# Second head mixing in seven chunks of 64 keys instead of eight of 56 and 64 columns

## The chip, the cores and the metric

The kernel runs on one core of a Trainium2 chip. The metric is the device time of one execution in microseconds. Three executions of the kernel before took 852.56, 857.35 and 858.68 us; the median is 857.35 us. The profiled execution, from which all rows below come, took 857.05 us.

## The reference

Talking-heads attention, then an MLP with SiLU, in float32. B = 4 batches, 12 heads, 448 positions, head size 64; the MLP has 1792 rows, 768 inputs and 2048 hidden units (its weights come as float64).

```python
scores = scale * np.matmul(q, k.transpose(0, 1, 3, 2))
scores = np.einsum('bhij,hg->bgij', scores, w_pre)        # first mixing of the heads
attn = np.exp(scores - np.max(scores, axis=-1, keepdims=True))
attn = attn / (np.sum(attn, axis=-1, keepdims=True) + 1e-09)
attn = np.einsum('bhij,hg->bgij', attn, w_post)           # second mixing of the heads
attn = np.matmul(attn, v)
...
h = x @ w_in                                              # x: attn, heads side by side
return (h * (1.0 / (1.0 + np.exp(-h)))) @ w_out
```

The order in which the 448 keys are held is free, as long as the scores and the values have them in the same order: the maximum, the sum and the product with `v` all run over the keys.

## The kernel before

**Stages.** The attention comes first, up to about 436 us. In its course the MLP's float64 weights are turned into float32 by a generator (`convert`, lines 38 to 100), whose loads and stores (`cw`, `cg`) share the DMA queue of SP with the attention's. Then comes the MLP (lines 629 and 645 on PE), which the change doesn't touch.

**Groups and pairs.** The queries of a batch are cut into tiles of 120 or 100 rows. Within one, a group is 2 x 5 query rows: a half of its 128 partitions holds (row, head) pairs of five rows, 60 of 64 partitions used. There are 184 groups, worked through in 92 pairs. The main loop (from line 695) goes over the groups, in a written order for each step:

- `scores` (line 339) makes scores of two heads; ACT and DVE copy them out of PSUM (`st`), and SP's DMA rearranges them into `g` (line 351), where a partition is a (row, head).
- `mix_pair` (line 399) is the first mixing, in four quarters of the PE array, 64 rows by 64 columns each: rows r of the array belong to one half of the partitions, columns c to one half of the output. DVE takes the negative maximum (line 405), ACT the exponential with its sum (line 409), into `e`, 128 x 448.
- `bound_sums`, `norm_pair` (lines 418 to 425) make 1/sum on DVE and, on POOL, `wr`: the weights of the second mixing over the sum.
- `mix_pair_again` (line 437) is the second mixing: the stationary operand is a piece of `e` (64 rows by 64 or 56 keys), the moving one is `wr` (64 x 60). A matmul of float32 is recorded as two instructions. For each of the two groups of a pair and each of `NJ` = 4 blocks of 112 keys there are four matmuls, one in each quarter: rows `s`, columns `c`. Column half `c` = 0 takes 64 keys, of which the last 8 are not its own, half 1 takes the next 56. The output `pa` has two banks of PSUM, one for each `s`.
- `put_pair` (line 446) copies `pa` out on ACT into `at`: 120 partitions hold 56 keys, 8 rows of a gap and 56 keys.
- `values` (line 368) multiplies `at` by `v`, 120 rows for each of four blocks; the gap rows of `v` are zeroed.

**Keys and values in SBUF.** Keys come by `load_k_pair` (line 249), 112 partitions of four keys each, are transposed on PE by `prep_k` (line 269) against the identity and split into two parts, `kh` on ACT and `kl` on DVE. Partition p holds keys 4p to 4p + 3, so column j * 112 + p of the transposed keys is key 4p + j. Values come by `load_v_quad` (lines 251 to 261), four heads at once, in two transfers of 56 partitions. The same four tiles `v4` also serve as the landing place of keys, so the gap rows, partitions 56 to 63 (zeroed as 32 to 63), are zeroed on POOL again when keys have been there since (line 256).

**Order.** All loads of the attention are issued by SP, in order of the program; `put` (line 469) fixes the step at which each is issued, some steps ahead of its use. On PE, POOL, DVE and ACT the order is the program's too.

Of the kernel before, what the change touches and what calls it, by code (L numbers as in the profile page):

```python
# [8 lines left out]
F32 = mybir.dt.float32  # L9
# [13 lines left out]
def raw(ap):  # L23

    return ap.bitcast(F32)
# [78 lines left out]
def talking_heads_then_silu_mlp(  # L104
# [11 lines left out]
    nc = tc.nc  # L116
    ctx.enter_context(tc.manual_schedule())
    B, H, S, D = q.shape
# [3 lines left out]
    RH = R // 2  # L122
    GP = 128
    HP = GP // 2
    GH = RH * H
    G0 = HP - GH
    JT = 112
    NJ = S // JT
    JH = JT // 2
    KV = 64 + JH  # L130
    HH = H // 2
    TQ = 12 * R
    LEAD = 4
# [15 lines left out]
    ident = const.tile([128, 128], F32, name="ident")  # L149
# [18 lines left out]
    def pool(name, bufs, stack=ctx, **kw):  # L168
        return stack.enter_context(tc.tile_pool(name=name, bufs=bufs, **kw))
# [5 lines left out]
    v2_p = pool("v2", 4, late, side="right")  # L175
    a_p = pool("a", 2, late, side="right")
# [16 lines left out]
    pa = ps_a.tile([128, 2, 512], F32, name="pa", tag="pa")  # L193
    turns = []

    def bank(p, name):
        if p is ps_a:
            turns.append(name)
            return pa[:, len(turns) % 2]
        return p.tile([128, 512], F32, name=name, tag="bank")  # L200

    v_tiles = [v2_p.tile([KV, 4, NJ, D], F32, name="v4", tag="v4") for _ in range(4)]
    zeroed = []
    g_tiles = [p.tile([GP, 12, S], F32, name="g", tag="g") for p in g_ps]

    def load_weights():
# [31 lines left out]
    def load_k_pair(b, h, queues=(nc.sync, nc.sync)):  # L238
        if h >= 4 if b == 0 else h // 4 != 1:
            x = (b * H + 8) // 4 % 4 if b else h // 4 - 1  # L240
            if x in zeroed:
                zeroed.remove(x)
            t = v_tiles[x][:JT, h % 4:h % 4 + 2].rearrange("p i j d -> p (i j d)")
            t = t.rearrange("p (j i d) -> p j i d", i=2, j=NJ)
        else:
            t = nat.tile([JT, NJ, 2, D], F32, name="kn", tag="kn")
        kns[b, h] = t
        for i in range(2):
            queues[i].dma_start(out=t[:, :, i, :], in_=k[b, h + i].rearrange("(p j) d -> p j d", p=JT))

    def load_v_quad(b, h):
        x = (b * H + h + 8) // 4 % 4
        t = v_tiles[x]
        if x not in zeroed:
            zeroed.append(x)
            nc.gpsimd.memset(t[32:64], 0.0)
        src = v[b, h:h + 4].rearrange("i (c p j) d -> c p i j d", c=2, p=JH)
        for c in (1, 0):
            nc.sync.dma_start(out=t[64 * c:64 * c + JH], in_=src[c])
        for i in range(0, 4, 2):  # L260
            vs[b, h + i] = t[:, i:i + 2]


    def prep_k(b, h):

        pt = bank(banks[0], "pt")
        kn = kns.pop((b, h))
        for j in range(NJ):
            nc.tensor.transpose(pt[:, j * JT:(j + 1) * JT], kn[:, j].rearrange("p h d -> p (h d)"), ident[:JT, :JT])

        kh, kl = ks[b, h] = [k2_p.tile([128, S], F32R, name=x, tag=x) for x in ("kh", "kl")]

        def take_high():
            nc.scalar.copy(out=kh, in_=pt[:, :S])

        def take_low():
            nc.vector.tensor_sub(out=kl, in0=pt[:, :S], in1=raw(kh))
        return [(take_high, take_low)]
# [101 lines left out]
    class Group:  # L380
# [47 lines left out]

        def mix_pair_again(self, other):

            for x, g in enumerate((self, other)):
                half = pa[:, :, x * 256:x * 256 + NJ * GH]
                for j in range(NJ):
                    for s, c in ((0, 0), (1, 1), (0, 1), (1, 0)):
                        rows = slice(HP * s, HP * (s + 1))
                        m = JH if c else 64
                        nc.tensor.matmul(  # L437
                            half[64 * c:64 * c + m, s, j * GH:(j + 1) * GH],
                            lhsT=g.e[rows, j * JT + c * JH:j * JT + c * JH + m], rhs=g.wr[rows], start=True, stop=True)

        def put_pair(self):
            if self.slot == 0:
                ats[self.n] = a_p.tile([KV, NJ, H, TQ], F32, name="at", tag="at")
            o, np, p = self.place()
            o += 2 * p * R
            nc.scalar.copy(  # L446
                out=ats[self.n].rearrange("p j g t -> p (j g) t")[:, :, o:o + 2 * R].rearrange("p x (c i) -> p x c i", i=RH),
                in_=pa[:KV].rearrange("p s (g w) -> p (s g) w", g=2)[:, :, :NJ * GH].rearrange("p c (x i) -> p x c i", i=RH))

    seq = [(b, ti) for b in range(B) for ti in range(len(tiles))]  # L450
    kns, qns, ks, vs, qs, gs, ats = {}, {}, {}, {}, {}, {}, {}
# [9 lines left out]
    at = lambda i: groups[i] if 0 <= i < len(groups) else None  # L461
# [13 lines left out]
    for n in range(1, len(seq)):  # L475
        p0, p1 = first[n - 1], first[n]
        spread = (0, 0, 0, 0, 2, 2) if n == 1 else (-6, -5, -4, -2, -1, 0) if p1 - p0 == 12 else (-6, -5, -4, -3, -2, -1)
        for h in range(0 if n > 1 else 2 * NE, H, 2):
            i = p0 + spread[h // 2]
# [7 lines left out]
    for n, (b, ti) in enumerate(seq):  # L487
        if n:
            p0 = first[n - 1]
            if n > 2:  # L490
                put(first[n - 2], lambda n=n: load_q(n)[0](), lead=7, w=2.1)
            for hg, i in ((0, p0 - 9), (1, p0 - 8)):
                if n > 1:
                    put(i, prep_q, n, hg)
            if ti == 0:
                c0 = first[n - 2]
                for h, i, lead in zip(range(0, H, 2), (0, 1, 3, 5, 7, 9), (10, 10, 11, 12, 5, 6)):
                    put(c0 + i, load_k_pair, b, h, lead=lead, w=1.2)
                    put(c0 + i, prep_k, b, h)
        if ti == 0:  # L500
            for h in range(0, H, 4):
                put(first[n] + ((5, 6, 8) if n else (15, 16, 18))[h // 4], load_v_quad, b, h, lead=2, w=1.8)
# [10 lines left out]
    def keep_busy(n):  # L513
        p = bank(ps_a, "busy")
        for _ in range(n):
            nc.tensor.matmul(p[:, :128], lhsT=ident, rhs=ident, start=True, stop=True)
# [9 lines left out]
    for h in range(0, 6, 2):  # L526
        load_k_pair(0, h, (nc.sync, nc.scalar))
    loads[1]()
    for h in range(6, H, 2):
        load_k_pair(0, h)  # L530
    steps = [(prep_q, 0, 0), (prep_k, 0, 0), (prep_k, 0, 2)]
    for h in range(0, H, 2):
        if h + 4 < H:
            steps.append((prep_k, 0, h + 4))
        steps += [(scores, 0, h)]
        if h == 0:
            steps.append((prep_q, 0, 1))
# [3 lines left out]
    for j, (what, *args) in enumerate(steps):  # L541
# [12 lines left out]
        if (what, *args) == (scores, 0, H - 2):  # L554
            for put_scores in second:
                put_scores()
    banks[:] = [ps_m]
    keep_busy(2)
    for i in range(0, LEAD, 2):
        at(i).mix_pair(at(i + 1), (ps_p, ps_m)[i // 2])  # L560
# [29 lines left out]
    def used(j):  # L590

        if j < 7 * NP:
            m, p = divmod(j, NP)
            return step_of["i", m, 0, 0], step_of["i", m, NU - 1, (4 * p + 3) // HC]
        m, f = divmod(j - 7 * NP, HF)
        return step_of["o", m, f // 2, 0], step_of["o", m, f // 2, NT2 - 1]

    for j in range(WB, len(parts)):
        s = max(used(j - WB)[1] + 1, used(j)[0] - 10)
# [80 lines left out]
    for f in range(HF):  # L680
        for m in range(7):
            if m:
                s = step_of["o", m - 1, f // 2, 0] + NT2 + 3 * (f % 2)
            else:
                s = o0 - 7 + 3 * f if f < 2 else o0 + NT2 * (f // 2 - 1) + 3 * (f % 2)
# [9 lines left out]
    for i in range(len(groups) + 1):  # L695
        g, new, old = at(i), at(i + LEAD), at(i - 1)
# [189 lines left out]
    for s, (kind, m, u, a) in enumerate(steps):  # L886
# [15 lines left out]
        p = None  # L902
        if kind == "o":
            if u == 0:
                accs[a] = bank(ps_h, "ph") if a < 4 else ps_t.tile([128, 512], F32, name="pt", tag="pt")
            p = accs[a]
            product(s, p)
        elif s >= len(phs):
            p = bank(ps_h, "ph")
# [18 lines left out]
        if kind == "i":  # L928
            n = u * HF + a
# [29 lines left out]
```

## Time and profile before

| | |
|---|---|
| median of 3 executions | 857.35 us |
| profiled execution | 857.05 us, span 855.3 us |
| PE busy | 811.6 us (95%) |
| PE weight loads | 661.6 us (77%) |
| DVE busy | 625.6 us (73%) |
| ACT busy | 511.0 us (60%) |
| POOL busy | 428.5 us (50%) |
| DMA | 132.90 MB, mean 155 GB/s |
| granted clock, mean | 0.986 |

An engine's busy time is the time in which at least one of its instructions ran; instructions that run side by side in quarters of the PE array count once. Weight loads (PEld) overlap matmuls. "Idle before" is the idle time of the engine ahead of an instruction, with what ended it. The chain of waits goes back from the last instruction to what released it, step by step; a work's share of it is the time that the end hung on that work. SPq is the queue on which SP issues transfers.

### The profile page before, as it was taken

What the parts mean: (1) busy time and instruction counts of PE and PEld (TensorE: products, weight loads), DVE (VectorE), ACT (ScalarE), POOL (GpSimd) and SP (SyncE); (2) the same over time, 40 slices, a digit from 0 to 9 for tenths busy, and PEclk for the clock granted to TensorE, in tenths of its full rate; (3) what the DMA queues carried; (4) which work ended last, traced back from release to release, by engine and by line L of the source; (5) the groups of instructions that cost most, each with busy time, mean ns of one, the idle gap of its engine ahead of it and who ended that gap; (6) DMA issues with size and microseconds to landing.
All of it is one profiled execution on the core that took longest, in us unless ns stands there. A gap on an engine that the chain in (4) does not pass through costs nothing.

```text
span 855.3 us, 27555 instructions
## 1 busy us (share of the span) xinstructions
PE 811.6 (95%) x11148; PEld 661.6 (77%) x11148; DVE 625.6 (73%) x1137; ACT 511.0 (60%) x1114; POOL 428.5 (50%) x693
## 2 busy tenths in 40 slices
PE   7898999799998999999899999999999999999997
PEld 5455666467665666666599999998989999999996
DVE  5553867467775777675778798999998888787343
ACT  4675878578886888787756554224676533433330
POOL 6131536355553554563877588457644435433440
PEclk9899999899999999999999999999999999999999
DMA  8668678887788786875535346335522122111133
GB/s 172 185 181 190 189 207 232 211 207 208 209 238 225 217 216 203 239 232 160 182 117 177 124 148 200 109 105 154 154 71 66 56 73 90 52 55 56 56 121 130
DMA packets 156839, 132.90 MB, mean 155 GB/s; under 512 B 52164, under 2 KB 150448, under 8 KB 156712
## 3 DMA queue, kind: packets, MB, share of 16 engines
q1 hardware_dynamic: 154339, 129.29, 53.3%
q8 instruction: 88, 1.44, 0.7%
q10 hardware_dynamic: 1956, 1.19, 0.6%
q0 software_dynamic: 416, 0.66, 0.3%
q14 instruction: 40, 0.32, 0.1%
HBM read 64.01 MB, written 27.53 MB: 107 GB/s over the span
## 4 chain that ended last, share of the span: by engine, by line
PE 71%; DVE 12%; DMA 6%; ACT 4%; issue 3%; POOL 2%; SPq 1%; ACTq 1%; DVEq 0%; POOLq 0%
PE ph L645 17%; PE ph L629 12%; PE pt L629 9%; PE pa L437 9%; PE po L368 7%; PE pp L399 7%; PE pqk L339 7%; DMA g<-st 3%; DVE op L652 2%; ACT e L409 1%; DVE nm L405 1%; DVE g L836 1%; DVE cg L92 1%; ACT at L446 1%; DVE g L838 1%
## 5 line engine op out<-in xcount | busy, mean ns | idle before, releaser
L616 POOL TENSOR_TENSOR wl<-wl,wh 128x384 fp32r<-128x384 f32 (+1 forms) x98 | 144.1, 1487 | 124.7 <-ACT wh L615 119.7
L425 POOL TENSOR_SCALAR wr<-wpost,r 128x60 f32<-128x60 f32 x184 | 72.7, 409 | 179.2 <-DVE r L422 131.6
L405 DVE TENSOR_REDUCE nm<-pp 128x1 f32<-128x448 f32 x184 | 106.1, 619 | 75.1 <-PE pp L399 74.6
L645 PE MATMUL ph<-op,wh 128*128 128x448 f32 x672 | 155.6, 367 | 2.7 <-DVE g L846 1.8
L409 ACT ACTIVATE e<-pp,nm 128x448 f32<-128x448 f32 x184 | 115.6, 633 | 46.6 <-DVE nm L405 44.0
L645 PEld LDWEIGHTS ph<-op,wh 128*128 128x128 f32 x672 | 125.3, 188 | 15.6 <-DVE g L846 2.1
L437 PEld LDWEIGHTS pa<-wr,e 64*64 64x64 f32 (+1 forms) x5888 | 96.4, 131 | 47.4 <-issue 29.2
L437 PE MATMUL pa<-wr,e 64*64 64x60 f32 (+1 forms) x5888 | 108.5, 218 | 16.7 <-ACT at L446 7.4
L66 POOL TENSOR_TENSOR cg<-cw,cg 128x256 f32<-128x256 f32 x96 | 75.7, 788 | 73.8 <-DVE cw L63 70.6
L399 PE MATMUL pp<-g,wpre 64*64 64x448 f32 x736 | 102.4, 573 | 8.3 <-ACT e L409 5.6
L446 ACT COPY at<-pa 120x960 f32<-120x960 f32 x92 | 90.0, 978 | 3.5 <-PE pa L437 3.5
L368 PE MATMUL po<-at,v 120*64 120x120 f32 (+1 forms) x1536 | 89.0, 271 | 2.1 <-DMA v<-in_v 1.2
L368 PEld LDWEIGHTS po<-at,v 120*64 120x64 f32 x1536 | 78.5, 141 | 15.4 <-issue 6.6
L645 PE MATMUL ph<-op,wl 128*128 128x448 f32 x336 | 86.6, 366 | 0.0
L344 DVE COPY st<-pqk 120x448 f32<-120x448 f32 (+1 forms) x89 | 54.8, 617 | 34.3 <-PE pqk L339 19.2
L90 ACT ACTIVATE cg<-cg,ebias 128x256 int32<-128x256 int32 x96 | 49.6, 517 | 39.8 <-DVE cg L86 38.6
L615 ACT CAST wh<-wl 128x384 fp32r<-128x384 f32 (+1 forms) x98 | 52.1, 556 | 33.1 <-DMA wl<-wi_dram 26.1
L92 DVE SCALAR_TENSOR_TENSOR cg<-cw,cg 128x256 int32<-128x256 int32 x96 | 55.4, 577 | 18.0 <-ACT cg L90 17.7
L645 PEld LDWEIGHTS ph<-op,wl 128*128 128x128 f32 x336 | 63.0, 188 | 5.5 <-POOL wl L616 0.5
L339 PEld LDWEIGHTS pqk<-kh,qh 64*120 64x120 f32 (+1 forms) x186 | 18.8, 174 | 43.2 <-issue 15.9
L346 ACT COPY st<-pqk 120x448 f32<-120x448 f32 (+1 forms) x89 | 48.1, 540 | 6.5 <-DMA g<-st 4.9
L399 PEld LDWEIGHTS pp<-g,wpre 64*64 64x64 f32 x736 | 23.2, 133 | 33.2 <-ACT e L409 14.5
(141 smaller groups left out, 1621.9 us busy)
## 6 DMA issues: line engine op xcount, KB each, us to landing
g<-st SPq DMA_DIRECT2D x132, 210.0 KB
cw<-in_moe_w_in SPq DMA_DIRECT2D x48, 256.0 KB
cw<-in_moe_w_out SPq DMA_DIRECT2D x48, 256.0 KB
wi_dram<-cg SPq DMA_DIRECT2D x24, 448.0 KB
wo_dram<-cg SPq DMA_DIRECT2D x24, 448.0 KB
wl<-wi_dram SPq DMA_DIRECT2D x42, 256.0 KB
wl<-wo_dram SPq DMA_DIRECT2D x56, 192.0 KB
g<-st SPq DMA_DIRECT2D x48, 175.0 KB
```

Source lines behind the costliest of these rows:

```text
L66: nc.gpsimd.tensor_mul(out=e, in0=m, in1=e)
L339: nc.tensor.matmul(ps[i][:m, :S], lhsT=q_[rows, hh, :m], rhs=k_[rows], start=(step == 0), stop=(step == 2))
L368: nc.tensor.matmul(po[i * D:(i + 1) * D, c * m:(c + 1) * m], lhsT=vs[b, h][:, i, j, :], rhs=ats[n][:, j, h + i, :m], start=(j == 0), stop= ...
L399: nc.tensor.matmul((self, other)[r].p[HP * c:HP * (c + 1), :S], lhsT=wpre[rows], rhs=gs[self.n][rows, o // R + c * np + p, :], start=True, ...
L405: nc.vector.tensor_reduce(out=self.nm, in_=self.p[:GP, :S], axis=AX.X, op=ALU.max, negate=True)
L409: nc.scalar.activation(out=self.e, in_=self.p[:GP, :S], func=AF.Exp, bias=self.nm, scale=1.0, accum_out=sums)
L425: nc.gpsimd.tensor_scalar(out=g.wr, in0=wpost.rearrange("p g i -> p (g i)"), scalar1=r[:, i:i + 1], scalar2=1.0, op0=ALU.mult, op1=ALU.mult)
L437: nc.tensor.matmul(half[64 * c:64 * c + m, s, j * GH:(j + 1) * GH], lhsT=g.e[rows, j * JT + c * JH:j * JT + c * JH + m], rhs=g.wr[rows], s ...
L446: nc.scalar.copy(out=ats[self.n].rearrange("p j g t -> p (j g) t")[:, :, o:o + 2 * R].rearrange("p x (c i) -> p x c i", i=RH), in_=pa[:KV] ...
L616: nc.gpsimd.tensor_sub(out=wl, in0=raw(wl), in1=raw(wh))
L629: nc.tensor.matmul(p[:, :W2], lhsT=x, rhs=w, start=(g == 0 and n == 0), stop=(g == FG - 1 and n == len(todo) - 1))
L645: nc.tensor.matmul(p[:, :T], lhsT=w, rhs=x, start=(n == 0), stop=(n == len(todo) - 1))
```

## The change

The keys are cut into seven chunks of 64. Chunks 0 to 2 lie on column half 0, chunks 4 to 6 on half 1, and chunk 3 on half 0 for the first group of a pair and on half 1 for the second. So the last four matmuls of a pair, one in each quarter, do chunk 3 of both groups, and a pair has 28 matmuls, not 32. The places of `pa` that belong to chunk 3 and are not written (half 1 of the first group, half 0 of the second) are zeroed once at the start, by two memsets on DVE; the copy takes them along, so `at` has zeros there. `at` and the tiles of values have 128 partitions. Chunk 3 of the values is in both halves of a tile, so a quad comes in three transfers, and no rows have to be zeroed.

The order of the keys changes with it: value partition p of a half holds keys 7p + n, chunk n. Keys are now loaded with 112 consecutive keys for each j, partition p holding key 112j + p; the transposes write their columns with a stride, so that key 7p + n stands at column 64n + p.

```diff
-    JH = JT // 2
-    KV = 64 + JH
+    KC = S // 64
...
-    v_tiles = [v2_p.tile([KV, 4, NJ, D], F32, name="v4", tag="v4") for _ in range(4)]
-    zeroed = []
+    v_tiles = [v2_p.tile([128, 4, NJ, D], F32, name="v4", tag="v4") for _ in range(4)]
...
     def load_k_pair(b, h, queues=(nc.sync, nc.sync)):
...
-            queues[i].dma_start(out=t[:, :, i, :], in_=k[b, h + i].rearrange("(p j) d -> p j d", p=JT))
+            queues[i].dma_start(out=t[:, :, i, :], in_=k[b, h + i].rearrange("(j p) d -> p j d", p=JT))
 
     def load_v_quad(b, h):
         x = (b * H + h + 8) // 4 % 4
         t = v_tiles[x]
-        if x not in zeroed:
-            zeroed.append(x)
-            nc.gpsimd.memset(t[32:64], 0.0)
-        src = v[b, h:h + 4].rearrange("i (c p j) d -> c p i j d", c=2, p=JH)
-        for c in (1, 0):
-            nc.sync.dma_start(out=t[64 * c:64 * c + JH], in_=src[c])
+        src = v[b, h:h + 4].rearrange("i (p n) d -> p i n d", n=KC)
+        nc.sync.dma_start(out=t[64:, :, :NJ - 1], in_=src[:, :, NJ:])
+        nc.sync.dma_start(out=t[64:, :, NJ - 1], in_=src[:, :, NJ - 1])
+        nc.sync.dma_start(out=t[:64], in_=src[:, :, :NJ])
...
     def prep_k(b, h):
...
+        cols = pt[:, :S].rearrange("p (n j a) -> p j a n", n=KC, j=NJ)
         for j in range(NJ):
-            nc.tensor.transpose(pt[:, j * JT:(j + 1) * JT], kn[:, j].rearrange("p h d -> p (h d)"), ident[:JT, :JT])
+            nc.tensor.transpose(cols[:, j], kn[:, j].rearrange("p h d -> p (h d)"), ident[:JT, :JT])
...
         def mix_pair_again(self, other):
 
-            for x, g in enumerate((self, other)):
-                half = pa[:, :, x * 256:x * 256 + NJ * GH]
-                for j in range(NJ):
-                    for s, c in ((0, 0), (1, 1), (0, 1), (1, 0)):
-                        rows = slice(HP * s, HP * (s + 1))
-                        m = JH if c else 64
-                        nc.tensor.matmul(
-                            half[64 * c:64 * c + m, s, j * GH:(j + 1) * GH],
-                            lhsT=g.e[rows, j * JT + c * JH:j * JT + c * JH + m], rhs=g.wr[rows], start=True, stop=True)
+            quarters = ((0, 0), (1, 1), (0, 1), (1, 0))
+            todo = [(x, s, c, j) for x in range(2) for j in range(NJ - 1) for s, c in quarters]
+            for x, s, c, j in todo + [(c, s, c, NJ - 1) for s, c in quarters]:
+                g, rows = (self, other)[x], slice(HP * s, HP * (s + 1))
+                n, w = j + NJ * c if j < NJ - 1 else j, x * 256 + j * GH
+                nc.tensor.matmul(
+                    pa[64 * c:64 * (c + 1), s, w:w + GH], lhsT=g.e[rows, 64 * n:64 * (n + 1)], rhs=g.wr[rows],
+                    start=True, stop=True)
 
         def put_pair(self):
             if self.slot == 0:
-                ats[self.n] = a_p.tile([KV, NJ, H, TQ], F32, name="at", tag="at")
+                ats[self.n] = a_p.tile([128, NJ, H, TQ], F32, name="at", tag="at")
...
-                in_=pa[:KV].rearrange("p s (g w) -> p (s g) w", g=2)[:, :, :NJ * GH].rearrange("p c (x i) -> p x c i", i=RH))
+                in_=pa.rearrange("p s (g w) -> p (s g) w", g=2)[:, :, :NJ * GH].rearrange("p c (x i) -> p x c i", i=RH))
...
     banks[:] = [ps_m]
+    for x in range(2):
+        nc.vector.memset(pa[64 * (1 - x):64 * (2 - x), :, x * 256 + (NJ - 1) * GH:x * 256 + NJ * GH], 0.0)
     keep_busy(2)
```

## Rows read from the trace of the kernel before

**Rows 1.** Busy time by stretch: us, PE, PEld, DVE, ACT, POOL, granted clock, DMA share, GB/s.

```profile
32.00:436.00 404.00, 376.01 (x8762) 252.84 (x8762) 272.19 (x646) 310.19 (x745) 198.27 (x458) 0.98 0.75 207
...
200.00:245.00 45.00, 43.84 (x1004) 29.96 (x998) 33.94 (x81) 37.14 (x88) 21.20 (x52) 1.00 0.73 209
56.00:86.00 30.00, 25.42 (x563) 16.56 (x559) 11.62 (x27) 17.69 (x42) 7.68 (x20) 0.94 0.86 197
145.00:170.00 25.00, 19.67 (x401) 11.98 (x398) 12.26 (x30) 14.75 (x36) 7.68 (x21) 0.92 0.85 224
250.00:285.00 35.00, 31.41 (x727) 20.88 (x721) 21.16 (x53) 24.88 (x62) 14.35 (x36) 0.95 0.91 232
345.00:375.00 30.00, 27.74 (x681) 18.61 (x682) 20.98 (x53) 23.08 (x57) 16.08 (x38) 1.00 0.85 243
```

**Rows 2.** The chain of waits from 32 to 436 us, shares by line.

```profile
by line: PE pa L437 18.1%; PE po L368 14.8%; PE pp L399 14.4%; PE pqk L339 14.1%; DMA g<-st 6.6%; issue 4.3%; ACT e L409 2.8%; DVE nm L405 2.7%; ACT at L446 2.2%; PE pt L269 1.7%; DMA qn<-in_q 1.7%; DMA v<-in_v 1.4%; SPq L249 1.2%; POOL wr 
```

**Rows 3.** Groups by line and form: shapes, count, busy us, mean ns, idle before.

```profile
L437 PE MATMUL pa<-wr,e 64*64 64x60 f32 x2944 | 108.5, 221 | 14.8 <-ACT at L446 7.4 <-issue 4.8 <-POOL cg L66 1.3
...
L437 PE MATMUL pa<-wr,e 64*56 64x60 f32 x2944 | 98.8, 216 | 1.9 <-issue 1.9
L437 PEld LDWEIGHTS pa<-wr,e 64*64 64x64 f32 x2944 | 96.4, 135 | 46.7 <-issue 28.4 <-POOL cg L66 5.0 <-POOL r L418 4.7
...
L437 PEld LDWEIGHTS pa<-wr,e 64*56 64x56 f32 x2944 | 85.7, 127 | 0.7 <-issue 0.7
```

**Rows 4.** Timeline of one pair's burst: start, duration, engine, line, count.

```profile
303.48 1.16 PE L437 MATMUL pa<-wr,e 64*64 64x60 f32 x64 [0.47 <-ACT at L446]
```

**Rows 5.** Lines 437 and 256: idle time ahead by reason; the memsets.

```profile
  issue: 35.8, 73
...
  POOL v L256: 2.3, 4
...
L256 POOL MEMSET v<- x6: 943/943/947, 55.7 to 348.9; 32x1024 f32 x6
```

**Rows 6.** Pieces of the chain around two memsets: start, duration, what.

```profile
55.72 0.95 POOL v L256
...
56.99 5.74 DMA v<-in_v
...
142.47 0.95 POOL v L256
143.42 0.10 issue
143.52 1.16 PE pa L437 x59
```

**Rows 7.** Value transfers on SP: min/median/max ns; then SP's timeline around 140 us.

```profile
L259 SPq DMA_DIRECT2D v<-in_v x24: 331/452/3354, 56.4 to 357.5; - x24
...
56.38 0.96 SPq L259 DMA_DIRECT2D v<-in_v  x2
...
140.31 3.46 SPq L259 DMA_DIRECT2D v<-in_v  x2
143.86 0.39 SPq L47 DMA_DIRECT2D cw<-in_moe_w_in  x1
```

**Rows 8.** DMA from 63 to 73 us; busy times from 303.4 to 304.7 us.

```profile
DMA packets 4505, 1.77 MB, mean 177 GB/s; under 512 B 3719, under 2 KB 4504, under 8 KB 4504
...
q1 hardware_dynamic: 4504, 1.75, 101.8%
...
303.40:304.70 1.30, 1.22 (x65) 1.19 (x66) 1.30 (x4) 1.30 (x4) 0.60 (x2) 1.00 0.98 336
```

**Rows 9.** Issues of keys, transposes, copies, value matmuls, a memset on DVE.

```profile
L249 SPq DMA_DIRECT2D v<-in_k x31: 573/633/2272, 2.7 to 302.7; - x31
...
L446 ACT COPY at<-pa 120x960 f32<-120x960 f32 x92 | 90.0, 978 | 3.5 <-PE pa L437 3.5
L368 PE MATMUL po<-at,v 120*64 120x120 f32 x1152 | 70.1, 277 | 1.2 <-DMA v<-in_v 1.2
L269 PE MATMUL pt<-ident,v 112*128 112x112 f32 x60 | 9.0, 272 | 0.4 <-DMA v<-in_k 0.4
...
16.92 0.11 DVE L227 MEMSET wpre<- 128x64 f32 x1
```

More of the change, by code (lines that the diff above doesn't have):

```diff
@@ L240, in load_k_pair @@
             x = (b * H + 8) // 4 % 4 if b else h // 4 - 1
-            if x in zeroed:
-                zeroed.remove(x)
             t = v_tiles[x][:JT, h % 4:h % 4 + 2].rearrange("p i j d -> p (i j d)")
```

## The prediction

> **What bounds the kernel now.** I read the busy times by stretch first. Between 32 and 436 us, where the attention with its second mixing runs, PE is busy for 376.0 of 404 us; ACT, the next, for 310.2. In the calm stretch from 200 to 245 us PE is busy for 43.8 of 45 us at a granted clock of 1.00 [rows 1]. The rest of the kernel, from 436 us on, contains nothing that the change touches. So TensorE sets the pace here, with one exception: there are four stretches, one for each batch, in which the DMA engines are at 0.85 to 0.91 of their capacity and PE loses time (31.4 of 35 us busy in one, 25.4 of 30 in another) [rows 1]. The keys and values are loaded there.
>
> The chain of waits for the same 404 us says how much of each work the end really hangs on: the second mixing (line 437) has 18.1% of it, so 73 us, and score transfers 6.6%, 27 us [rows 2]. By lines the second mixing keeps PE busy for 108.5 us in all [rows 3]. So 0.67 of its busy time lies on the path; in the other third something else (a transfer, ACT or DVE) was later, and a shorter burst of matmuls there only waits longer.
>
> **The burst of one pair.** 5888 records of line 437 are 64 for each of 92 pairs, that is 16 in each quarter of the array, and each quarter works through its own. The quarters with 64 weight columns are busy for 108.5 us, those with 56 for 98.8, so the narrow half is done 0.105 us earlier in each pair and the wide half ends the burst [rows 3]. A whole burst takes 1.16 us [rows 4]; less one matmul of 0.22 us, 15 steps take 0.94 us, 63 ns each.
>
> The change puts 64 columns everywhere, but 14 records in a quarter, not 16. If the wide quarter still sets the step, two steps go: 125 ns for a pair, 11.5 us for 92. Bounds: if the burst went by the number of matmuls alone, an eighth of 108.5, 13.6 us. If the four quarters shared one path for weights, it would go by columns: 16 x (64+64+56+56) = 3840 against 14 x 256 = 3584, 6.7%, or 7.2 us. I take 11.5, since the two halves show different ends, which a shared path would not give. Times 0.67 on the path: **-7.7 us**.
>
> The weight loads of the two widths last 135 and 127 ns [rows 3], 8 ns for 8 columns. The Trainium skill (TensorE: Matmul & The Clock Gate, LDWEIGHTS) has a load go by its columns alone, at 1.2 per ns, so 53 ns for 64. The trace's step of 63 ns is longer than that, and its difference by width agrees. By the page's figure alone the two steps would be 107 ns, 9.8 us for all pairs, and by the same share 6.6 on the path.
>
> **Zeroing of the gap rows.** Six memsets of 0.94 us on POOL go. PE and its loads waited 2.3 us behind them [rows 5]. On the chain one stands at 142.47 us, straight ahead of a burst, with 0.95 us; another at 55.72 leads into a value transfer, whose first half had already left SP at 56.38 behind other transfers [rows 6]. I count the first: **-1.0 us**; bounds 0 and -2.3. On SP the second half of a load had to wait for the memset: the two issues from 140.31 took 3.46 us where 0.45 each is usual [rows 7]. What stood behind it on SP then was a weight load of the later part, whose landing nobody was waiting for on the path, so nothing for that.
>
> **Values.** A quad of heads is now three transfers, not two, twelve times. Chunk 3 is loaded twice: 64 KB more in each quad, in pieces of 256 bytes. Nearest rows: a full stretch in which most packets are that small moved 177 GB/s, one with large ones 336 [rows 8]. So 64 KB take 0.2 to 0.37 us, 4.4 us over the kernel at most; below zero it may come out if 64 partitions are spread better over the 16 engines than 56. One more issue on SP is 0.45 us at the median, 3.35 at worst [rows 7]. In the first batch the chain runs through SP and the value transfer (5.74 us from 56.99) [rows 6], so three quads x 0.37 there and one more issue of 0.45; the other nine quads mostly lie under PE work. I take **+1.5 us**, bounds -1 and +4.4, and the worst SP case as a rival.
>
> **Keys, transposes, and the rest.** Pieces of keys stay at 256 bytes and as many issues of 0.63 us [rows 9]; only their order in memory changes. Nothing in the trace shows that order alone; queries, whose pieces lie far apart too, share the stretch of [rows 8] with them. I take 0; if a fetch of 112 KB (0.63 us at 177 GB/s) took half as long again, 12 of the 48 in the prologue or the first batch would add 3.7 us. The 96 transposes of keys (0.27 us each) [rows 9] now write their columns 64 apart in PSUM. No matmul of the trace writes so. Zero if the stride is free, which I take because no row of the trace shows PE slowed by where it writes; if they took double, the 1.7% of the path that they hold [rows 2] would come on top, +6.9 us. Copies out of PSUM have 128 partitions, not 120, and the same 960 elements in each (0.98 us); value matmuls run over 128 rows, not 120, with the same columns [rows 9]. Both at 0: a transpose over 112 rows (0.27 us, 112 columns) and a value matmul over 120 (0.28, 120 columns) [rows 9] leave no room for a price per row. Two memsets of PSUM on DVE once before the first mixing: the nearest is 0.11 us [rows 9], so **+0.3 us**. The chain passes DVE there, so nothing hides them. There are 736 fewer matmul records and as many fewer weight loads; "issue" stands as a reason of idle time ahead of line 437 with 35.8 us [rows 5], most of it on the load side alone. I take nothing, bound -2.
>
> **What is late next.** Where PE was just ahead of ACT (the exponentials, the copy of `at`), a shorter burst hands the path to it: 310 of 404 us busy [rows 1] leave room on average, not in every pair. I take back +0.4.
>
> Sum: -7.7 - 1.0 + 1.5 + 0.3 + 0.4 = -6.5. Against the profiled execution's own 857.05 us (span 855.3) that is 850.5. The median of the runs is 857.35, 0.3 above, so the same forecast, 0.8% under it.
>
> **Rivals.**
> A. As summed: 850.5, own range 846 to 854.5. For it: the share of the path, and four stretches that belong to the DMA engines. 56%.
> B. The saving counts in full. Work that PE finishes early in a waiting stretch would shorten the queue behind it, and the waits for POOL go too: 857 - 11.5 - 2.3 + 1.8 = 845, between 843 and 848. For it: PE at 0.97 in calm stretches. Against: 27 us of the path are score transfers. 25%.
> C. Transfers or transposes take it back: value bytes at +4.4 and the key order at +3.7, or strided transposes at +6.9, give 856 to 858, and the change can't be told from nothing. 11%.
> D. Slower: SP. It issues in order, and score transfers, on which the first mixing waits, stand behind the values. If every third issue met the worst hold, 2.9 us over the median [rows 7], twelve would add 35 us: 885. It decides from 1.3 us a quad on, for then 16 us outweigh the gain and 1%. Against: the median of the 24 issues is 0.45 us [rows 7], and SP loses its waits for the memset. 8%.
> The change does what it says: the records of line 437 must drop by an eighth, so no chance is kept for the opposite.
>
> **Chances.** About 1% (8.6 us: under 848.8 or over 865.9) is what a measurement of this kernel can tell from no change. Faster: nearly all of B, and a seventh of A's range: 0.31. Slower: D, 0.08. Within: 0.61. The range 844 to 858 leaves out D, the top of C and the foot of B, some 17%.
>
> **What would show it.** 5152 records of line 437, all 64 wide; the burst of a pair at 1.03 to 1.05 us, and line 437 busy for about 97 us in all. If it stays near 1.1, the quarters share something. No POOL memset of `v`. 36 value issues; the stretch from 56 to 86 us not shorter than before, the one from 200 to 245 shorter by 1.2 us. If PE's idle time between 32 us and the end of attention grows by as much as its busy time falls, C holds; if SP's value issues last over 1 us at the median, D. The forecast is wrong if the transposes or the copies last longer, or if PE's clock falls in stretches where it was 1.00.

## The result, and the profile after

The changed kernel is **slower by 0.6%**: 863.68 us at the median of 22 runs beside 861.19 us for the kernel before on the same chips, ratio 1.0058, 95% interval 1.0036 to 1.0080. The ratio is taken from fast runs alone; the medians over all runs stand at 1.0029 and the means at 1.0034, so the loss is 2.5 to 5.0 us. Forecast were 850.5 us and a range from 844 to 858. The forecast counted from 857.35 us, the median of three executions; over 22 that median is 3.8 us higher, which is bad luck of the starting point. What has to be explained is the change beside the kernel before: up to +5.0 us where -6.5 was forecast. The profiled execution after took 859.51 us, with a span of 857.8 us; it is the shortest of the 22.

The busy times by stretch of the kernel after answer to [rows 1] (columns as there):

```profile
32.00:436.00 404.00, 372.08 (x8018) 244.66 (x8020) 271.93 (x650) 309.81 (x749) 191.28 (x453) 0.97 0.77 209
200.00:245.00 45.00, 44.42 (x976) 29.69 (x975) 35.11 (x82) 37.59 (x90) 22.11 (x54) 1.00 0.76 219
56.00:86.00 30.00, 23.25 (x518) 15.06 (x518) 13.15 (x31) 18.52 (x46) 5.12 (x19) 0.96 0.92 198
145.00:170.00 25.00, 19.93 (x392) 12.84 (x384) 12.40 (x30) 15.04 (x38) 7.70 (x21) 0.91 0.93 213
250.00:285.00 35.00, 31.06 (x640) 20.18 (x638) 19.92 (x48) 23.87 (x60) 14.37 (x36) 0.95 0.89 220
345.00:375.00 30.00, 25.76 (x534) 16.29 (x528) 18.70 (x49) 21.18 (x53) 13.58 (x33) 0.94 0.89 224
```

In the calm stretch PE is as busy as before, 44.4 of 45 us. In three of the four stretches with loads the DMA share rises (0.86 to 0.92, 0.85 to 0.93, 0.85 to 0.89; from 250 to 285 us it is 0.89 after 0.91), and in the first and the last of them PE is busy for 2 us less. In the last its granted clock is 0.94, where it was 1.00. From 145 to 170 us the DMA engines are busier than before and move less.

The chain of waits from 32 to 436 us, by line, answers to [rows 2]: the second mixing went from 18.1 to 15.5%, score transfers from 6.6 to 8.3%.

```profile
by line: PE po L363 16.3%; PE pa L431 15.5%; PE pp L394 15.2%; PE pqk L334 13.3%; DMA g<-st 8.3%; issue 3.3%; ACT e L404 3.3%; DVE nm L400 2.7%; ACT at L440 2.3%; PE pt L264 2.1%; ACT qh L314 1.7%; DMA v<-in_v 1.4%; DMA qn<-in_q 1.3%; DMA c
```

The groups by line and form answer to [rows 3] and [rows 9]. All matmuls of the mixing are 64 wide, an eighth fewer, and busy for 98.5 us; copies and value matmuls last as long as before, transposes 0.28 where they took 0.27 us.

```profile
L431 PE MATMUL pa<-wr,e 64*64 64x60 f32 x5152 | 98.5, 222 | 14.3 <-ACT at L440 8.4 <-issue 4.0 <-POOL cg L66 1.4
...
L363 PE MATMUL po<-at,v 128*64 128x120 f32 x1152 | 69.7, 276 | 1.7 <-DMA v<-in_v 1.7
L264 PE MATMUL pt<-ident,v 112*128 112x112 f32 x60 | 9.4, 282 | 0.1
...
L440 ACT COPY at<-pa 128x960 f32<-128x960 f32 x92 | 90.0, 978 | 3.3 <-PE pa L431 3.3
```

PE's timeline shows a full burst at 1.04 us, where [rows 4] have 1.16. It also shows the start of the mixing: the warming matmuls write the PSUM bank that DVE comes to zero only at 27.68 us, and wait for that; the first burst begins at 34.23 us, 2.2 us later than before. The last row is DVE's.

```profile
28.23 0.68 PE L510 MATMUL pa<-ident 128*128 128x128 f32 x4 [1.91 <-DVE pa L553]
28.84 4.66 PE L394 MATMUL pp<-g,wpre 64*64 64x448 f32 x24
...
34.23 1.04 PE L431 MATMUL pa<-wr,e 64*64 64x60 f32 x56
```

```profile
27.68 0.41 DVE L553 MEMSET pa<- 64x120 f32 x2
```

The three value transfers of a quad on SP (min/median/max ns), against one row of [rows 7]:

```profile
L251 SPq DMA_DIRECT2D v<-in_v x12: 596/683/2662, 58.6 to 355.2; - x12
L252 SPq DMA_DIRECT2D v<-in_v x12: 595/642/1627, 59.4 to 357.9; - x12
L253 SPq DMA_DIRECT2D v<-in_v x12: 596/608/1671, 60.1 to 358.7; - x12
```

### The profile page after: what moved, and what is told of

It reads as the page before. It is cut to its first block, busy times and chain, and to the rows that moved or that the text cites. A ratio compares the mean times of both kernels' runs of the same rounds, so it can differ in the third digit from the quotient of the medians.

```text
span 857.8 us, 26009 instructions
## 1 busy us (share of the span) xinstructions
PE 808.6 (94%) x10412; PEld 654.0 (76%) x10412; DVE 624.5 (73%) x1139; ACT 510.0 (59%) x1114; POOL 422.3 (49%) x687
## 4 chain that ended last, share of the span: by engine, by line
PE 70%; DVE 11%; DMA 8%; ACT 5%; issue 2%; SPq 2%; POOL 1%; ACTq 1%; DVEq 0%; POOLq 0%
PE ph L641 17%; PE ph L625 12%; PE pt L625 9%; PE po L363 8%; PE pa L431 7%; PE pp L394 7%; PE pqk L334 7%; DMA g<-st 4%; ACT e L404 2%; DVE op L648 1%; DVE g L832 1%; DVE nm L400 1%; DVE cg L92 1%; ACT at L440 1%; ACT qh L314 1%
## 5 line engine op out<-in xcount | busy, mean ns | idle before, releaser
L431 PEld LDWEIGHTS pa<-wr,e 64*64 64x64 f32 x5152 | 86.1, 135 | 45.5 <-issue 27.4
L394 PE MATMUL pp<-g,wpre 64*64 64x448 f32 x736 | 104.8, 582 | 9.2 <-ACT e L404 6.7
L431 PE MATMUL pa<-wr,e 64*64 64x60 f32 x5152 | 98.5, 222 | 14.3 <-ACT at L440 8.4
L440 ACT COPY at<-pa 128x960 f32<-128x960 f32 x92 | 90.0, 978 | 3.3 <-PE pa L431 3.3
L363 PE MATMUL po<-at,v 128*64 128x120 f32 (+1 forms) x1536 | 89.9, 272 | 1.8 <-DMA v<-in_v 1.7
L363 PEld LDWEIGHTS po<-at,v 128*64 128x64 f32 x1536 | 79.4, 142 | 14.5 <-issue 9.2
L334 PE MATMUL pqk<-kh,qh 64*120 64x448 f32 (+1 forms) x186 | 47.5, 462 | 7.1 <-ACT st L341 5.6
```

The source lines that it names most:

```text
L334: nc.tensor.matmul(ps[i][:m, :S], lhsT=q_[rows, hh, :m], rhs=k_[rows], start=(step == 0), stop=(step == 2))
L363: nc.tensor.matmul(po[i * D:(i + 1) * D, c * m:(c + 1) * m], lhsT=vs[b, h][:, i, j, :], rhs=ats[n][:, j, h + i, :m], start=(j == 0), stop= ...
L394: nc.tensor.matmul((self, other)[r].p[HP * c:HP * (c + 1), :S], lhsT=wpre[rows], rhs=gs[self.n][rows, o // R + c * np + p, :], start=True, ...
L431: nc.tensor.matmul(pa[64 * c:64 * (c + 1), s, w:w + GH], lhsT=g.e[rows, 64 * n:64 * (n + 1)], rhs=g.wr[rows], start=True, stop=True)
L440: nc.scalar.copy(out=ats[self.n].rearrange("p j g t -> p (j g) t")[:, :, o:o + 2 * R].rearrange("p x (c i) -> p x c i", i=RH), in_=pa.rear ...
```

## The experiments

Ratios are to the kernel before, run beside each kernel on the same chip; 0.001 is 0.86 us. Brackets hold the 95% interval.

**The changed kernel, one part altered.** First the memsets behind the warming matmuls (e1), then from there the values in two transfers of 1024-byte pieces (e2), the keys fetched in the old order (e3), and both (e4). In e3 and e4 values and keys don't match.

```diff
 e1
-    for x in range(2):
-        nc.vector.memset(pa[...], 0.0)
     keep_busy(2)
+    for x in range(2):
+        nc.vector.memset(pa[...], 0.0)
 e2 (chunk 3 is slot 0 of half 1)
-        nc.sync.dma_start(out=t[64:, :, :NJ - 1], in_=src[:, :, NJ:])
-        nc.sync.dma_start(out=t[64:, :, NJ - 1], in_=src[:, :, NJ - 1])
+        nc.sync.dma_start(out=t[64:], in_=src[:, :, NJ - 1:])
 e3
-... in_=k[b, h + i].rearrange("(j p) d -> p j d", p=JT))
+... in_=k[b, h + i].rearrange("(p j) d -> p j d", p=JT))
```

> The changed kernel with one thing moved: the two memsets of PSUM stand behind the two warming matmuls (line 516 of before), not ahead of them. Theory M (in the changed kernel these matmuls, and the first mixing behind them, wait for the memsets, which are last on DVE: PE idle for 1.91 us, then 1.1 us more at the lower clock): PE's idle time there is gone, the first burst of the second mixing starts 2 us earlier than in the changed kernel, ratio to before 1.003 to 1.004 instead of 1.0058. Rival D (the DMA queue sets when the first tile of scores is there, so what is won at the start is lost by the first batch's loads): first burst 2 us earlier, ratio still 1.005 to 1.006.

> The kernel of the run ahead, with chunk 3 of the values at the other end of half 1 (first of four, not last), so that each half of a quad is one transfer in pieces of 1024 bytes: two transfers, not three, the same bytes, the same number of matmuls. Theory V (three value transfers a quad hold SP for 1.93 us, not 0.9, and put 256-byte pieces in the way of the score transfers, so that the tile after the loads of each batch starts 2 to 3 us late): 4 to 7 us faster than the run ahead, ratio to before 0.995 to 0.999. Theory K (the keys' scattered order costs it): no difference to the run ahead, within 1.5 us.

> The first of these runs with the keys fetched as in the kernel before, four keys in a row for each partition; the keys then stand in another order than the values, which is the part of the computation that changes. Theory K: 4 to 7 us faster than the first of these runs, ratio 0.995 to 0.999. Theory V: within 1.5 us of it, ratio 1.002 to 1.005.

> Both: values in two transfers and keys fetched as before (so keys and values stand in different orders). With all that the change added to the transfers taken back but the 64 KB of each quad, the shorter bursts should be left: by V or K alone the same as the better of the two runs, 0.995 to 0.999; if both cost, 0.989 to 0.994. A theory C, that the shorter bursts give nothing at all because transfers set the pace of every tile: 1.000 to 1.003.

Measured: e1 1.0052 [1.0013, 1.0092], e2 1.0057 [1.0029, 1.0085], e3 1.0019 [0.9988, 1.0051], e4 1.0023 [0.9992, 1.0055]. The wait for the memsets is gone from e1's trace, and the total doesn't show it: at most a few tenths of a percent. Three transfers or two, with or without 256-byte pieces, makes no difference that shows (0.4 us, uncertain by 2.8). The old order of keys gives 0.0034 on the mean of both pairs, 2.9 us, with an uncertainty as large as itself. So neither theory V nor theory K, with 4 to 7 us each, came true; e4 stands in the range of theory C, which e5 tests.

**The kernel before, one part of the change alone.** e5 does 28 of the 32 matmuls of a pair (one block of the first group is left out), e7 the new fetch of keys. e6 is e1 with the last four matmuls done twice.

```diff
 e5
-                for j in range(NJ):
+                for j in range(NJ - 1 + x):
```

> The kernel before with one thing left out: the first group's last block of 112 keys in the second mixing (four matmuls of 32 in each pair), so bursts are as short as after the change and nothing else is changed (that block of the result is not computed). Theory G (the gain of the bursts is real, and the change's other parts take it away): 0.989 to 0.993 of before, mean granted clock as before, 0.985. Theory C (shorter bursts make PE wait longer for the score and value transfers, and its clock falls in those waits, so that the gain is lost by itself): 0.996 to 1.001, clock 0.975 to 0.980.

> The changed kernel with the memsets behind the warming matmuls (run e1) and with the last four matmuls of each pair done twice, so bursts are as long as before the change and all its other parts stay. Theory G: 1.012 to 1.016 of before (e1's 1.0052 and the 10 us of the bursts). Theory C: 1.003 to 1.008, not different from e1, and a granted clock above e1's 0.975.

> The kernel before with the keys' fetch of the changed kernel alone (partition p holds keys p, p + 112 and so on; keys and values then stand in different orders). If the scattered fetch costs something by itself: 1.002 to 1.005 (the two pairs of runs so far put it at 2.3 us). If not: 0.998 to 1.001.

Measured: e5 **0.9924** [0.9891, 0.9957], e6 1.0074 [1.0039, 1.0109], e7 1.0013 [0.9980, 1.0045]. So the gain of the shorter bursts is real in the kernel before, 6.5 us, as theory G had it. The other signs came out as theory C had them. The mean granted clock fell in e5, to 0.980 beside 0.985. And e6, with long bursts again, is only 0.0022 over e1, 1.9 us (uncertain by 4.5), inside theory C's range and below G's, at a clock of 0.980 beside e1's 0.975. So the same bursts may be worth less in the changed kernel than the 6.5 us; the two values differ by 4.6, uncertain by 5.4. The keys' order alone isn't measurable in the kernel before. The change as a whole is 0.0134 above e5: some 11.5 us are lost in other parts.

**An earlier issue of values.** e8 is e2, e9 the kernel before, with the first two value quads of the first batch issued six and four steps earlier.

```diff
-                put(first[n] + ((5, 6, 8) if n else (15, 16, 18))[h // 4], load_v_quad, ...)
+                put(first[n] + ((5, 6, 8) if n else (9, 12, 18))[h // 4], load_v_quad, ...)
```

> Run e2 (memsets behind, values in two transfers) with the first two value quads of the first batch issued six and four groups earlier, where the DMA engines are less busy. In e2 PE waits 4.2 us for values at 61 us. If the first batch's waits are where the gain goes: that wait is gone, 2 to 5 us faster than e2, ratio 0.999 to 1.003. If the wait only moves to the score transfers behind: same as e2, 1.004 to 1.007.

> The kernel before with one edit: the first two value quads of the first batch are issued six and four steps earlier; nothing else. If the earlier issue repairs something that only the change made late, the kernel before gains little by it: its wait for values at 61.6 us was 1.25 us, so a ratio of 0.998 to 1.002. If it is an improvement of its own that the change only happened to carry (the loads spread out of the full stretch), the kernel before gains as much as the changed kernel did, 0.8%: 0.990 to 0.994.

Measured: e8 0.9975 [0.9946, 1.0004], 0.0082 under e2; e9 0.9978 [0.9944, 1.0013]. The same step is worth 7 us to the changed kernel and, at its middle value, 2 to the kernel before: the values of the first batch have become late (in e2 PE waits 4.2 us for them, in the kernel before 1.2).

**The values alone.** e10 and e11 are e5 with 64 partitions and 512 KB a quad in two transfers, strided as in the change or from solid rows; e12 is e5 without the POOL memsets; e13 is e11 without the 64 KB that the change adds, in transfers of 64 and 48 partitions, with value matmuls over 112 rows. Keys and values don't match in e10, e11 and e13; in e12 gap rows hold old keys.

```diff
 e10
+        src = v[b, h:h + 4].rearrange("i (p n) d -> p i n d", n=7)
+        nc.sync.dma_start(out=t[64:], in_=src[:, :, 3:])
+        nc.sync.dma_start(out=t[:64], in_=src[:, :, :4])
 e11
+        for c in (1, 0):
+            src = v[b, h:h + 4, 192 * c:192 * c + 256].rearrange("i (p n) d -> p i n d", n=4)
+            nc.sync.dma_start(out=t[64 * c:64 * c + 64], in_=src)
 e13
+        for c, m in ((1, 48), (0, 64)):
+            src = v[b, h:h + 4, 256 * c:256 * c + 4 * m].rearrange("i (p n) d -> p i n d", n=4)
+            nc.sync.dma_start(out=t[64 * c:64 * c + m], in_=src)
```

> The kernel before with seven blocks of matmuls per pair (0.9924 in the run before) and the values alone fetched as the change fetches them, in two transfers: 64 partitions, 1024 bytes out of every 1792, 64 KB more per quad; the memset of gap rows stays, the order of the keys and the transposes too (so values and keys don't match). If the way in which the values lie in memory is what the change lost, this loses 5 to 7 us of the gain: 0.998 to 1.001. If the values cost nothing and the loss is with the strided transposes, the 128-row copies and matmuls, or the memset that went: 0.991 to 0.994.

> As the run beside it, with the same 64 partitions and the same 512 KB per quad in two transfers, but from solid stretches of memory (rows 0 to 255 and 192 to 447, four rows after one another to a partition). If the stride of 1792 bytes is what costs, this stays with the seven blocks alone: 0.991 to 0.994, and the strided run stands 5 us above it. If it is the 64 KB more per quad, or 64 partitions in place of 56, both lose alike: 0.997 to 1.001.

> The kernel before with seven blocks of matmuls per pair and without the six memsets of gap rows on POOL in the loop (two stand in the prologue; the gap rows hold keys later). If the memsets cost PE time, as the prediction had it, 0.2 to 1 us less than with them: 0.991 to 0.992. If they held the second transfer of a quad back to the good of the score transfers, so that their going is a part of the loss: 0.995 to 0.998.

> As the run with values from solid stretches (seven blocks, keys as before), but without the 64 KB more per quad: 64 partitions in one transfer, 48 in the other, 448 KB as in the kernel before, in pieces of 1024 bytes; the value matmuls take 112 rows (values and keys don't match). If the bytes cost the gain: back at 0.990 to 0.994, about 8 us under the solid run. If it is that a transfer covers 64 partitions and not 56: it stays at 1.000 to 1.003. Between, if both.

Measured: e10 **1.0014** [0.9978, 1.0050], e11 **1.0023** [0.9988, 1.0058], e12 0.9912 [0.9877, 0.9948], e13 **0.9965** [0.9931, 0.9999]. The values alone take back all that e5 had gained, some 8 us (uncertain by 4). The stride has no part in it that shows. Without the 64 KB, 5.0 us of it return (0.0058, uncertain by 0.0049). The rest between e13 and e5, 0.0041, is within its uncertainty of 0.0047.

How the bytes cost time the traces show only in part. First the stretch from 56 to 86 us, in e5, e11 and e13 (columns as in [rows 1]):

```profile
56.00:86.00 30.00, 25.50 (x531) 16.83 (x530) 14.64 (x34) 19.61 (x48) 8.18 (x23) 0.94 0.90 212
```

```profile
56.00:86.00 30.00, 23.64 (x458) 14.59 (x452) 11.82 (x27) 17.26 (x41) 7.43 (x20) 0.89 0.97 192
```

```profile
56.00:86.00 30.00, 25.10 (x463) 15.27 (x462) 12.17 (x28) 17.97 (x44) 8.10 (x21) 0.88 0.90 205
```

With the 64 KB more per quad the DMA engines are at 0.97 and move 192 GB/s, not 212; without them they are back at 0.90. SP's timeline in the same stretch, again e5, e11, e13, and then e12:

```profile
60.79 3.22 SPq L249 DMA_DIRECT2D v<-in_k  x4
...
74.55 5.54 SPq L351 DMA_DIRECT2D g<-st  x6
```

```profile
61.21 6.15 SPq L249 DMA_DIRECT2D v<-in_k  x4
...
78.77 5.18 SPq L351 DMA_DIRECT2D g<-st  x6
```

```profile
61.48 4.39 SPq L249 DMA_DIRECT2D v<-in_k  x4
...
75.93 5.18 SPq L351 DMA_DIRECT2D g<-st  x6
```

```profile
61.96 6.21 SPq L247 DMA_DIRECT2D v<-in_k  x4
...
78.44 5.17 SPq L349 DMA_DIRECT2D g<-st  x6
```

The first score transfers behind the loads leave SP 4.2 us later in e11 than in e5. Four key issues take 6.15 us there, where e5 needed 3.22. But e12, which has the 448 KB and the partitions of e5 and the lowest ratio so far, shows 6.21 us and 78.44 us too, so this hold comes without the added bytes, and it isn't shown that the bytes cost their time by it. Last the waits for score transfers from 32 to 436 us (engine, line, us in all, times, longest), in e5, e11 and e13:

```profile
DVE st L344 <- DMA g<-st: 12.8, 9, 3.7
...
ACT st L346 <- DMA g<-st: 5.8, 7, 2.7
```

```profile
DVE st L344 <- DMA g<-st: 19.2, 8, 6.9
ACT st L346 <- DMA g<-st: 13.1, 6, 5.4
```

```profile
DVE st L344 <- DMA g<-st: 16.6, 10, 4.0
...
ACT st L346 <- DMA g<-st: 6.7, 6, 2.5
```

18.6, 32.3 and 23.3 us: the copies that fill the next score buffers wait for the transfers before them, and PE waits for those copies. Over the traces of all experiments this holds on average: with short bursts the same two waits add up to 19.7 to 40.2 us in the eight kernels with the 64 KB (the changed one, e1 to e4, e8, e10, e11), 32.5 in the mean, and to 18.6 to 26.2 in the six without (e5, e12 to e16), 22.5 in the mean. The four with long bursts (before, e6, e7, e9) have 13.0 to 18.8; e6, the one of them with the 64 KB, has 13.0. (The profiled execution of e11 took 865.23 us, its median is 862.52; the totals are taken from the ratios.)

**A version without the second transfer of chunk 3.** e14 is e1 with that chunk copied by POOL from the lower to the upper partitions; e15 issues the first quads early too, and the copy one step earlier than e14; e16 is e15 with the old order of keys (keys and values don't match).

```diff
 e14
-        nc.sync.dma_start(out=t[64:, :, NJ - 1], in_=src[:, :, NJ - 1])
...
+    def double_v(b, h):
+        t = v_tiles[(b * H + h + 8) // 4 % 4]
+        nc.gpsimd.tensor_copy(out=t[64:, :, NJ - 1], in_=t[:64, :, NJ - 1])
...
                 put(p0 + i, values, n - 2, p, 2)
+                if seq[n - 2][1] == 0:
+                    put(p0 + i, double_v, seq[n - 2][0], 2 * p, lead=1)
```

> The changed kernel (memsets of PSUM after the warming matmuls) without the second transfer of chunk 3: POOL copies that chunk from the lower to the upper half of the partitions, one copy of 64x256 per quad, before the values are used; 448 KB per quad, two transfers. If the bytes cost the gain: 0.994 to 0.998, 6 to 9 us under the changed kernel's 1.0052 in this form. If not: 1.002 to 1.006.

> As the run with the copy on POOL, and with the first two value quads of the first batch issued earlier. By bytes: that run less some 2 us, what the kernel before had from the same step, so 0.991 to 0.996. If the bytes are not it: 0.996 to 1.000, as the earlier issue alone gave 0.9975.

> As the run with copy and earlier issue, with the keys fetched in the order of the kernel before (so keys and values don't match). If the order of the keys costs the 2 to 3 us that earlier pairs of runs suggest, this is 0.003 under that run; if the order is free, within 0.001 of it.

Measured: e14 0.9979 [0.9942, 1.0016], 0.0073 or 6.3 us under e1; **e15 0.9902 [0.9863, 0.9941]**, 854.96 us, faster than both kernels; e16 0.9907 [0.9878, 0.9937]. So the 64 KB cost the changed kernel about what they cost e11, 6.3 us (uncertain by 4.6) and 5.0 (uncertain by 4.2); e8 and e15, both with the early issue, are 6.3 us apart too (uncertain by 4.2). The order of the keys makes 0.0005 here, uncertain by 0.0049: no cost shows, but the 2.9 us aren't excluded. e15's copies are 4.9 us of POOL in all:

```profile
L259 POOL COPY v<-v 64x256 f32<-64x256 f32 x12 | 4.9, 410 | 1.7 <-DMA v<-in_v 1.0
```

SP issues the first late score transfers at 79.50 us in the changed kernel, at 77.85 in e1, at 77.91 in e14 and at 75.35 in e15:

```profile
79.50 5.21 SPq L346 DMA_DIRECT2D g<-st  x6
```

```profile
77.85 5.91 SPq L346 DMA_DIRECT2D g<-st  x6
```

```profile
77.91 5.19 SPq L349 DMA_DIRECT2D g<-st  x6
```

```profile
75.35 5.19 SPq L349 DMA_DIRECT2D g<-st  x6
```

The waits for score transfers in e1 and e14:

```profile
DVE st L339 <- DMA g<-st: 16.7, 10, 5.6
...
ACT st L341 <- DMA g<-st: 8.7, 4, 4.1
```

```profile
DVE st L342 <- DMA g<-st: 18.4, 12, 3.8
...
ACT st L344 <- DMA g<-st: 7.4, 6, 2.7
```

From e1 to e14, where the bytes go, neither SP's issue nor these waits (25.4 and 25.8 us) change, and the DMA share from 56 to 86 us stays at 0.94 and 0.93. So in this pair the way by which the bytes cost 6.3 us is not seen in the traces.

e14 is still 4.7 us above e5 (uncertain by 4.3), and the steps from e14 to e15 take off 6.6 us (uncertain by 4.6), so the first batch still loses time without the 64 KB. Whether by the 64 partitions to a transfer, the order of the keys or e14's later copy on POOL was not separated. e15 stands where e5 and e9 would together (0.9924 x 0.9978 = 0.9902): there nothing of the loss is left.

## Why the prediction was wrong, step by step

**Bursts, -7.7: right for the kernel before.** Bursts of 1.04 us and 5152 records, as said; 98.5 us busy, 97 expected. e5 measures the term at -6.5 us (-9.4 to -3.7), so the share of 0.67 on the path held there. In the changed kernel e6 measures it at -1.9, uncertain by 4.5, so that part of it may be lost again to the waits for transfers.

**Gap rows, -1.0: not contradicted.** e12 is 1.0 us under e5, uncertain by 4.

**Values, +1.5 with bounds -1 and +4.4: this step failed.** Measured is some 8 us (uncertain by 4), of which the added bytes are 5.0 (e11 less e13) to 6.3 (e1 less e14). The error was not in the rate: 12 x 64 KB are 0.79 MB, and at the 197 GB/s of the stretch [rows 1] that is 4.0 us, near the upper bound that I had. It was in what I let count. I charged the first batch alone, 1.1 us and an issue, and said that "the other nine quads mostly lie under PE work". The same rows that I had called the exception, four stretches at 0.85 to 0.91 of DMA capacity, spoke against that overlap: at the middle values the bytes cost all of their transfer time and more. And the bound priced the values' own transfers alone; on average over the traces the score transfers come later too, and with them the copies of `st` on DVE and ACT.

What stays open is the way. Either the other nine quads were not hidden, or the first batch pays several times its own transfers. The profiled executions don't agree: e11 falls 5.0 us behind e5 up to the thirteenth copy of `at` and 11.0 up to the last, e1 falls 3.7 us behind e14 up to the thirteenth and 2.2 up to the last. e12, whose transfers are those of e5, is 4.0 us behind it at the thirteenth and 0.7 ahead at the last, so that such differences of single executions decide little.

The price by the size of pieces was misread as well. The 336 GB/s of [rows 8] were taken for large packets, but 224 of that row's 357 packets are under 512 bytes too, in a stretch of 1.3 us. Pieces of 256 bytes or of 1024 make no difference that shows (e1 and e2).

The runs also leave open whether 64 partitions to a transfer are worse than 56 (e13 less e5, +3.5 us, uncertain by 4). The Trainium skill (DMA: Bandwidth & Descriptors, Why a DMA increments its semaphore by 16 and not by 1) has a transfer use the largest number of engines up to 16 that divides its outer dimension, so 14 for 56 and 16 for 64. If more engines made a transfer quicker, the new form would gain; the ratios of e13 and e5 give no sign of it, and the engine of a packet isn't in these traces.

**Keys, 0 with +3.7: between.** 2.9 us with the 64 KB (e3, e4 against e1, e2, with an uncertainty of the same size), -0.4 without them and with the early issue (e16 against e15, uncertain by 4.2). Neither differs clearly from nothing. **Strided transposes, 0 with +6.9:** the transposes' rows are 0.28 and 0.27 us, so 0 stands for their own time; no run has them alone.

**Memsets on DVE, +0.3: mis-sized and without effect.** I priced their duration alone; it is 0.41 us. What counted was the PE wait of 1.91 us that they made, and 2.2 us at the first burst. But removing it (e1) changes the total by 0.0006, far inside the uncertainty; that the first batch's waits take it up is likely, not shown.

**What is late next, +0.4.** The wait of the mixing for the copy of `at` rose from 7.4 to 8.4 us, by more than the term but by little. On the chain it was not ACT (the copy at 2.2, then 2.3%) but the score transfers that took more (6.6, then 8.3%).

**Sum with measured terms:** -6.5 - 1.0 + 8 + 2.9 + 0.5 = +3.9, against +5.0 measured (0.0058 x 861; +2.5 by the medians of all runs). The difference is inside the terms' uncertainties. But the terms were measured beside different kernels, and need not add up.

**Rivals.** C named the right mechanism for the value bytes (that the key order takes its part is not shown), with both terms at their bounds, and came out at most at 858 because the value bound was 4.4. D had SP's order as the way in which score transfers get late. They do get late on average, but whether by SP's order is not shown, and the price was wrong: there is no worst hold at every third issue. Its sign, value issues above 1 us at the median, did not show: 683, 642 and 608 ns. Of the signs that I named, the stretch from 56 to 86 us "not shorter" held. From 32 us to the last copy of `at` (432.8 us, after 433.7) PE is busy for 3.1 us less and idle for 3.9 us more: sign of C. And the clock fell in a stretch where it was 1.00 (345 to 375 us, 0.94), one of the signs of a wrong forecast.

## What to carry to other kernels

Before bytes are added to save work on the busiest engine, ask in which stretches they will be moved. Where the DMA share is near 0.9, they can cost all of their transfer time and more: here 5 to 6 us, each value uncertain by over 4, for bytes that take an estimated 4.0 (0.79 MB at the 197 GB/s of [rows 1]). A copy on an engine with idle time, here 12 of 0.41 us on POOL, can be much cheaper than loading the same data twice. And a chain share of the whole (0.67 on the path) priced the shorter bursts well where nothing else was changed. It need not hold beside a change that makes transfers later, for then a saving on PE can end in a wait; e6 hints at that and doesn't decide it.

## What the runs showed of the hardware that was not expected

The DMA share says little of what is moved. From 56 to 86 us e11 moved 192 GB/s at a share of 0.97 where e5 moved 212 at 0.90, so a busy microsecond carried 16% less. It is not the added bytes alone: without them e14 moved 192 GB/s at 0.93, and e12 194 at 0.87. The mix of packets in the stretch was not held fixed.

The waits also cost clock. Four rows of e11, by stretches of 4 us, show the granted clock at 1.00 (2.4 GHz) while PE is busy for 1.21 of 4 us, then 0.73 and 0.84, part of these stretches at 1.2 GHz, after the wait, while PE is busy again:

```profile
60.00:64.00 4.00, 1.21 (x58) 0.94 (x56) 2.38 (x5) 1.93 (x6) 0.84 (x4) 1.00 1.05 199
64.00:68.00 4.00, 3.14 (x36) 2.52 (x40) 0.00 (x0) 0.54 (x3) 0.00 (x0) 0.73 1.07 152
68.00:72.00 4.00, 4.00 (x80) 2.04 (x76) 1.93 (x5) 2.83 (x7) 0.81 (x3) 0.84 0.92 168
72.00:76.00 4.00, 4.00 (x104) 2.88 (x100) 2.30 (x5) 3.15 (x9) 0.81 (x3) 1.00 1.25 167
```

Over all runs the mean granted clock was 0.985 for the kernel before, 0.980 for e5 and 0.974 for the changed one; no term of my sum had a price for a wait's effect on what comes after it. Which part of the lost time is clock and which is waiting was not separated.
